# Attention and a two-layer network in one kernel: where the network's steps, the products with v and the weight sums stand

## The chip, the cores and the metric

The kernel runs on one core of one Trainium2 chip. The metric is the device time of one execution in microseconds (us), the median of several runs. The engines that matter here are PE (TensorE, the matrix products), DVE (VectorE), ACT (ScalarE), POOL (GpSimd) and SP (SyncE, which here only issues transfers, DMAs). Each has its own queue of instructions, runs it in the order in which it is written, and waits at semaphores for the others.

## The reference

Per batch (8) and head (8) an attention over 576 tokens of 64 values with a decay, then per token a normalised two-layer network of 512, 2048 and 512 values:

```python
scores = scale * np.matmul(q, k.transpose(0, 1, 3, 2))
decay = cum[:, :, :, None] - cum[:, :, None, :]      # cum: running sum of log f
scores = np.where(causal, -1000000000.0, scores + decay)
attn = np.exp(scores - np.max(scores, axis=-1, keepdims=True))
attn = attn / (np.sum(attn, axis=-1, keepdims=True) + 1e-09)
x = np.matmul(attn, v)                               # heads side by side: (8, 576, 512)
xn = (x - mu) / np.sqrt(var + 1e-06) * g_ln
return x + np.maximum(xn @ w_ch1, 0.0) @ w_ch2
```

## The kernel before

**Slots.** Attention is cut into 256 slots, four per head: slot u works on head u // 4 and on a block of 128 query rows, t = 1 to 4 (t = 1 takes a first block of 64 rows along, t = 0). In its slot a block gets its scores (`qk_mm`, PE, tiles s), its softmax (`softmax_a` on DVE, `softmax_e` on ACT, `normalise` on DVE and POOL, tile p) and, one slot later, a copy into another buffer by DMA (`move`, tile pq). `LAG_MOVED = 4` slots after the scores PE transposes the block (`transpose_unit`, tiles tr), ACT copies the result (`transposed_hi`, tile ph) and DVE the low part of it (`transposed_lo`, tile pl). The product with v (`av_unit`, tile o, from vv, ph and pl) covers two blocks at a time and stands one slot after the second one's transposes, t = 2 or t = 4. `finish` and `finish_add` write o to xs, and every second head's xs goes to DRAM (xa, xb). Heads 0 to 13 are handled with a shorter lag and in other orders.

**Steps.** The network works on chunks of 256 tokens, 18 of them. For the first `PLAIN_CHUNKS = 12` a chunk takes 16 steps, one per 128 hidden values: `mm1` (12 matmuls of 256 columns: four blocks of w1, each in high and low parts), `mm1_high` and `mm1_low` (ACT and DVE, tile hh), and `mm2` (6 matmuls of 512 columns), which stands in the next slot that is reached. A slot holds at most one step. From slot `EVEN_FROM = 70` on, `credit` spreads the steps that are left evenly over the slots that are left, so that some slots have none. `moe.limit` says which chunks' tokens are finished, and `Moe.fetch` loads and splits the next chunk (tiles xr, x) from 8 steps before it begins.

**Wide part.** The last six chunks are done after attention, as `WIDE = 3` times 512 tokens in `wide_part`, with 7 products for 8 in the first layer (`Wide.order`). They need sums and differences of blocks of w1; `weight_sums` makes these in 80 pieces (8 times 10; mostly POOL, some ACT), the last piece of each ten being `keep`: four stores to DRAM (sd) on SP. One piece stands in every slot from `SUMS_FROM = 120`. `wide_start` loads and prepares the first 512 tokens, in the last five slots, which have no scores any more.

**Order.** All queues are written by hand: a slot runs the letters of a string in `ORDERS`, from slot 56 on `WwAthQFlMSPNgreamLRDBZ`. A is the product with v, the transposes and the scores, dealt among each other by `dealt`; h and l are the copies of the transposes; M is `mm1`, N is `mm2` of the step before; S, e and B are the softmax; F and a finish o; P prepares a coming head (casts, subtractions and the loads kl, raw, vr, and xq, whose rows come from the cast); R is `moe.rest` (loads and splits of chunks); D is `move`; Z a piece of the sums. PSUM has six banks in rotation for tr, s, o, h and xp.

Of the kernel before, what the change touches and what calls it, by code (L numbers as in the profile page):

```python
# [31 lines left out]
LAG, LAG_MOVED = 2, 4  # L32
MOVED = 14
PLAIN_CHUNKS = 12
WIDE = (NCHUNK - PLAIN_CHUNKS) // 2
PAIRS = FT // 2
EVEN_FROM = 70
SUMS_FROM = 120
# [27 lines left out]
def attn_moe(ctx: ExitStack, tc: tile.TileContext, qk, v, f, g, w1, w2, out):  # L66
# [387 lines left out]
    def transpose_unit(h, t):  # L454
        n = f"{h.n}"
        pt = rows_of(h, t)
        work_, todo = [], []

        def tr(out_, in_):
            m = in_.shape[0]  # L460
            if in_.dtype == F32R:
                todo.append(lambda: nc.tensor.transpose(out_.bitcast(F32R), in_, identr[:m, :m]))  # L462
            else:
                todo.append(lambda: nc.tensor.transpose(out_, in_, ident[:m, :m]))

        if t <= 2:
            if t == 1:
                h.ph1 = work.tile([P, 704], F32 if h.full else F32R, tag="ph1", bufs=1, name=f"ph1_{n}")
                h.pl1 = None if h.full else late.tile([P, 384], F32R, tag="pl1", bufs=1, name=f"pl1_{n}")
            ph = h.ph1  # L470
            pl = ph if h.full else h.pl1
            tp = bank(f"tr{n}_{t}")
            if t == 1:
                tr(tp[0:64, 0:128], rows_of(h, 0)[:, 0:D])
                tr(tp[0:64, 64:192], pt[:, 0:64])
                tr(tp[:, 192:320], pt[:, 64:192])
                work_.append((tp[0:64, 0:192], ph[0:64, 0:192], ph[64:128, 0:192]))
                work_.append((tp[:, 192:320], ph[:, 320:448], pl[:, 0:128]))
            else:
                tr(tp[0:64, 0:128], pt[:, 0:64])  # L480
                tr(tp[:, 128:256], pt[:, 64:192])
                tr(tp[:, 256:384], pt[:, 192:320])
                work_.append((tp[0:64, 0:128], ph[0:64, 192:320], ph[64:128, 192:320]))
                work_.append((tp[:, 128:384], ph[:, 448:704], pl[:, 128:384]))
        else:
            if t == 3:
                h.ph2 = work.tile([P, 9 * P], F32 if h.full else F32R, tag="ph2", bufs=1, name=f"ph2_{n}")
                h.pl2 = None if h.full else late.tile([P, 7 * P], F32R, tag="pl2", bufs=1, name=f"pl2_{n}")
            c = 0 if t == 3 else P
            ph = h.ph2[:, : 8 * P].rearrange("p (k c) -> p k c", k=4)[:, :, c : c + P]  # L490
            pl = None if h.full else h.pl2[:, : 6 * P].rearrange("p (k c) -> p k c", k=3)[:, :, c : c + P]
# [4 lines left out]
            work_.append((tp[0:64, 0, :], ph[0:64, 0, :], ph[64:128, 0, :]))  # L496
            work_.append((tp[:, 1:4, :], ph[:, 1:4, :], pl))
            if t == 4:
                tp = bank(f"tr{n}_4b")[:, :P]
                tr(tp, pt[:, 64 + 3 * P : 64 + 4 * P])  # L500
                work_.append((tp, h.ph2[:, 8 * P :], None if h.full else h.pl2[:, 6 * P :]))
        h.parts = work_
        return todo

    def transposed_hi(h, t):
        for tp, hi, lo in h.parts:
            nc.scalar.copy(out=hi, in_=tp)  # L507
# [58 lines left out]
    def dealt(t, u1, a, b, q):  # L566

        if t == 4 and q:
            return a[:5] + a[8:] + b[:2] + q[:1] + a[5:6] + b[2:] + q[1:2] + a[6:7] + q[2:3] + a[7:8] + q[3:]
        if t == 4:  # L570
            return a[:5] + a[8:] + b[:2] + a[5:6] + b[2:] + a[6:8]
        if t == 2:
            return a[:3] + a[4:] + b + a[3:4] + q
        return (a + b if u1 else b[1:] + b[:1]) + q
# [386 lines left out]
    def wide_start(u):  # L961

        w, k = wides[0], u - (len(slots) - LAG_MOVED - 1)
# [138 lines left out]
    slots += [None] * (LAG_MOVED + 1)  # L1102
# [14 lines left out]
    for u, slot in enumerate(slots):  # L1117
# [7 lines left out]
        def turn(more):  # L1125

            for lag in (LAG, LAG_MOVED):
                b = before(lag + more)
                if b is not None and hd[b[0]].lag == lag:
                    return b  # L1130
            return None

        av, av_t = None, 0
        if turn(1) is not None and turn(1)[1] in (2, 4):
            av, av_t = hd[turn(1)[0]], turn(1)[1]
# [11 lines left out]
        def piece(c):  # L1147
            tu = turn(0)
# [36 lines left out]
            elif c == "R":  # L1185
                moe.limit = min(PLAIN_CHUNKS, max(0, u - (LAG if u < 4 * MOVED else LAG_MOVED) - 1) // (4 * H) * S // C)
# [24 lines left out]
            elif c == "Z":  # L1211
                if u >= SUMS_FROM and sum_todo:
                    sum_todo.pop(0)()
                if slot is None:
                    wide_start(u)

        def prep():
# [13 lines left out]
            first = turn(0)  # L1231
# [4 lines left out]
            second = turn(1)  # L1236
# [5 lines left out]
    moe.limit = PLAIN_CHUNKS  # L1242
    while moe.left() > 0:
# [7 lines left out]
        moe.rest()  # L1251
    for _ in range(W2_LOW):
# [41 lines left out]
```

## Time and profile before

| | |
|---|---|
| device time, median of 3 runs | 1218.45 us (1218.02 to 1218.68) |
| the profiled execution | 1218.54 us, of which 1216.8 us from its first to its last instruction (the span) |
| PE busy | 1176.7 us, 97% of the span |
| DVE, ACT, POOL busy | 812.9, 669.8, 521.5 us (67%, 55%, 43%) |
| DMA | 249.62 MB, 205 GB/s in the mean |
| mean granted TensorE clock | 0.988 of full speed |

A matmul's end is modelled, so busy shares of PE also cover time in which it is only filling; what a matmul occupies is read from the starts of two that follow each other. Waits are idle time of an engine before an instruction, with the instruction or DMA that ended it. Where time is read from a timeline, the first number is the start in us from the span's start and the second the duration shown.

### The profile page before, as it was taken

To read this page: it belongs to the slowest core of one execution; us is meant where nothing else is said; L and a number is where in the kernel's file an instruction comes from. 1 tells how busy PE (TensorE), PEld (TensorE's weight loads), DVE (VectorE), ACT (ScalarE), POOL (GpSimd) and SP (SyncE) were. 2 spreads that over 40 slices of the span, in tenths; PEclk is the share of its full clock that TensorE was granted. 3 is DMA by queue.
4 is the path that set the end of the run, shared out by engine and by line. 5 is a ranking of instruction groups with operands and counts; after the bars stand their busy time and mean duration, and the time that the engine had idled before them with its cause. 6 is when DMAs were issued, how large, how long until landed. Compare 5 with 4: busy or idle time off the path is not lost. (4 is left out here: it accounts for less than half of the span.)

```text
span 1216.8 us, 26138 instructions
## 1 busy us (share of the span) xinstructions
PE 1176.7 (97%) x7996; PEld 1040.8 (86%) x7996; DVE 812.9 (67%) x2935; ACT 669.8 (55%) x1981; POOL 521.5 (43%) x633
## 2 busy tenths in 40 slices
PE   7998999999999999999999999999999999999998
PEld 5666889989898998888888888889998899898997
DVE  5787646676868777686777768686776635536433
ACT  5887645565666666566566666666664322223221
POOL 3568543444444556655665664444442202002000
PEclk8998999999999999999999999999999999999999
DMA  6778654666666677767777677667765646545542
GB/s 202 226 241 265 204 160 142 198 219 206 219 219 222 216 232 232 217 210 245 234 244 250 214 239 251 197 200 247 214 201 152 227 142 190 191 149 182 173 139 95
DMA packets 181916, 249.62 MB, mean 205 GB/s; under 512 B 39952, under 2 KB 111632, under 8 KB 181776
## 3 DMA queue, kind: packets, MB, share of 16 engines
q1 hardware_dynamic: 181776, 247.95, 64.7%
q8 instruction: 64, 1.05, 0.4%
q14 instruction: 76, 0.62, 0.1%
HBM read 166.90 MB, written 31.75 MB: 163 GB/s over the span
## 5 line engine op out<-in xcount | busy, mean ns | idle before, releaser
L428 POOL TENSOR_SCALAR p<-p,st 64x64 f32<-64x64 f32 (+4 forms) x320 | 172.1, 542 | 403.4 <-DVE st L427 156.4
L421 ACT ACTIVATE p<-p,st 64x64 f32<-64x64 f32 (+4 forms) x320 | 178.6, 559 | 117.9 <-DVE st L410 93.5
L634 PE MATMUL h<-x,w1h 128*128 128x256 f32 x768 | 222.3, 289 | 3.3 <-DVE xs L602 1.8
L635 PE MATMUL h<-x,w1h 128*128 128x256 f32 x768 | 218.7, 285 | 0.6 <-DVE x L619 0.3
L636 PE MATMUL h<-x,w1l 128*128 128x256 f32 x768 | 217.7, 283 | 0.0
L634 PEld LDWEIGHTS h<-x,w1h 128*128 128x128 f32 x768 | 146.9, 191 | 8.0 <-DVE xs L602 2.9
L507 ACT CAST ph<-tr 64x128 fp32r<-64x128 f32 (+4 forms) x416 | 117.3, 331 | 64.9 <-PE tr L462 43.9
L656 PE MATMUL acc<-w2h,hh 128*128 128x512 f32 x384 | 152.0, 396 | 0.0
L657 PE MATMUL acc<-w2s,hh 128*128 128x512 f32 x384 | 151.5, 395 | 0.0
L658 PE MATMUL acc<-w2h,hh 128*128 128x512 f32 x384 | 150.9, 393 | 0.0
L635 PEld LDWEIGHTS h<-x,w1h 128*128 128x128 f32 x768 | 147.1, 192 | 2.3 <-DVE x L619 1.5
L636 PEld LDWEIGHTS h<-x,w1l 128*128 128x128 f32 x768 | 147.1, 192 | 0.0
L410 DVE CUSTOM_DVE_ANT_0 p<-s,mask 64x64 f32<-64x64 f32 (+4 forms) x320 | 130.3, 420 | 19.7 <-DMA pq<-p 8.1
L642 ACT ACTIVATE hh<-h 128x256 fp32r<-128x256 f32 x192 | 73.6, 383 | 112.1 <-PE h L636 110.9
L1061 POOL TENSOR_TENSOR c<-u,s 128x256 f32<-128x256 f32 x24 | 17.7, 737 | 223.4 <-DVE u L1060 223.4
L512 DVE TENSOR_TENSOR ph<-tr,ph 64x192 fp32r<-64x192 f32 x208 | 62.6, 301 | 74.8 <-ACT ph L507 70.7
L374 PE MATMUL s<-hi 128*64 128x64 f32 x336 | 103.5, 314 | 4.0 <-DVE st L410 1.7
L647 DVE SCALAR_TENSOR_TENSOR hh<-h,hh 128x256 fp32r<-128x256 f32 x192 | 80.5, 419 | 33.1 <-ACT hh L642 31.5
L374 PE MATMUL s<-kl,xq 66*64 66x64 f32 x336 | 96.4, 291 | 3.8 <-DMA xq<-hi 3.6
L512 DVE TENSOR_TENSOR pl<-tr,ph 128x128 fp32r<-128x128 f32 x208 | 95.3, 458 | 4.6
L462 PE MATMUL tr<-identr,pq 128*128 128x128 f32 (+1 forms) x700 | 93.4, 233 | 2.9 <-DMA pq<-p 2.9
L658 PEld LDWEIGHTS acc<-w2h,hh 128*128 128x128 f32 x384 | 72.4, 189 | 16.5
(146 smaller groups left out, 2951.2 us busy)
## 6 DMA issues: line engine op xcount, KB each, us to landing
w2s<-w2d SPq DMA_DIRECT2D x192, 256.0 KB
raw<-in_qk_dram SPq DMA_DIRECT2D x56, 576.0 KB
s<-sd SPq DMA_DIRECT2D x96, 256.0 KB
wr<-in_w_dram SPq DMA_DIRECT2D x32, 512.0 KB
pq<-p SPq DMA_DIRECT2D x50, 288.0 KB
wide<-w2d SPq DMA_DIRECT2D x48, 256.0 KB
pq<-p SPq DMA_DIRECT2D x50, 224.0 KB
vr<-in_v_dram SPq DMA_DIRECT2D x64, 160.0 KB
```

What stands on the lines that cost most here:

```text
L374: todo.append(lambda: nc.tensor.matmul(*a, **k))
L410: nc.vector.tensor_tensor_reduce(out=pt[:m, a:z], in0=sp, in1=mask[:m, off + a : off + z], scale=-SCALE, scalar=3.0e38 if i == 0 else st[: ...
L421: nc.scalar.activation(pt[:m, :w], pt[:m, :w], AF.Exp, bias=st[:m, i : i + 1], scale=-1.0, accum_out=st[:m, 2:3])
L428: nc.gpsimd.tensor_scalar(out=pt[:m, :w], in0=pt[:m, :w], scalar1=st[:m, 3:4], scalar2=1.0, op0=ALU.mult, op1=ALU.mult)
L507: nc.scalar.copy(out=hi, in_=tp)
L512: nc.vector.tensor_tensor(out=lo, in0=tp, in1=hi.bitcast(F32), op=ALU.subtract)
L634: mm(ph, w1h[:, k, fs], c.x[k][:, 0, :], start=(k == 0), stop=False)
L635: mm(ph, w1h[:, k, fs], c.x[k][:, 1, :], start=False, stop=False)
L636: mm(ph, w1l[:, k, fs], c.x[k][:, 0, :], start=False, stop=(k == KT - 1))
L656: mm(c.acc[i], h[:, 0, ts_], w2h[:, j, :], start=(j == 0), stop=False)
L657: mm(c.acc[i], h[:, 0, ts_], low, start=False, stop=False)
L658: mm(c.acc[i], h[:, 1, ts_], w2h[:, j, :], start=False, stop=(j == FT - 1))
```

## The change

Fourteen chunks instead of twelve are done in steps, and two times 512 tokens instead of three by seven products. A step stands in every slot whose chunk is ready (`EVEN_FROM = 1000` is never reached). The product with v stands three slots after the second transposes instead of one (`AV_MOVED = 3`); the cast of v (`prep_v`), its load and the limit of the chunks move two slots with it, the loop gets two more slots at its end, and ph and pl are allocated where they are written (`places`) and no longer where the transposes stand, since the product with the old ones now stands in that same slot. `dealt` mixes the matmuls of a slot in other ways. The sums of w1 begin in slot 92 and stand in every second slot. `wide_start` moves from the last slots to the steps that are left after the loop.

```diff
 W2_WAIT = 2
 ALL = 2 * NCHUNK * FT + W2_WAIT
 LAG, LAG_MOVED = 2, 4
+AV, AV_MOVED = 1, 3
 MOVED = 14
-PLAIN_CHUNKS = 12
+PLAIN_CHUNKS = 14
 WIDE = (NCHUNK - PLAIN_CHUNKS) // 2
 PAIRS = FT // 2
-EVEN_FROM = 70
-SUMS_FROM = 120
+EVEN_FROM = 1000
+SUMS_FROM = 92
...
+    def places(h, t):
+
+        n, tp = f"{h.n}", h.banks[0]
+        if t == 1:
+            h.ph1 = work.tile([P, 704], F32 if h.full else F32R, tag="ph1", bufs=1, name=f"ph1_{n}")
+            h.pl1 = None if h.full else late.tile([P, 384], F32R, tag="pl1", bufs=1, name=f"pl1_{n}")
+        if t == 3:
+            h.ph2 = work.tile([P, 9 * P], F32 if h.full else F32R, tag="ph2", bufs=1, name=f"ph2_{n}")
+            h.pl2 = None if h.full else late.tile([P, 7 * P], F32R, tag="pl2", bufs=1, name=f"pl2_{n}")
...
+        return out_
+
     def transposed_hi(h, t):
+        h.parts = places(h, t)
         for tp, hi, lo in h.parts:
...
     def dealt(t, u1, a, b, q):
 
-        if t == 4 and q:
-            return a[:5] + a[8:] + b[:2] + q[:1] + a[5:6] + b[2:] + q[1:2] + a[6:7] + q[2:3] + a[7:8] + q[3:]
         if t == 4:
-            return a[:5] + a[8:] + b[:2] + a[5:6] + b[2:] + a[6:8]
+            return a[:5] + a[8:] + b[:1] + a[5:6] + b[1:2] + a[6:7] + b[2:3] + a[7:8] + b[3:] + q
+        if t == 2 and q:
+            return a[:3] + a[4:] + b[:2] + q[:1] + a[3:4] + b[2:] + q[1:]
         if t == 2:
-            return a[:3] + a[4:] + b + a[3:4] + q
-        return (a + b if u1 else b[1:] + b[:1]) + q
+            return a[:3] + a[4:] + a[3:4] + b
+        return (b if u1 else b[1:] + b[:1]) + q
 
...
-    def wide_start(u):
-
-        w, k = wides[0], u - (len(slots) - LAG_MOVED - 1)
+    def wide_start(k):
+
+        w = wides[0]
         if k == 0:
...
-    slots += [None] * (LAG_MOVED + 1)
+    slots += [None] * (LAG_MOVED + AV_MOVED)
...
-        def turn(more):
-
-            for lag in (LAG, LAG_MOVED):
-                b = before(lag + more)
+        def turn(more, more_moved):
+
+            for lag, k in ((LAG, more), (LAG_MOVED, more_moved)):
+                b = before(lag + k)
                 if b is not None and hd[b[0]].lag == lag:
                     return b
             return None
 
         av, av_t = None, 0
-        if turn(1) is not None and turn(1)[1] in (2, 4):
-            av, av_t = hd[turn(1)[0]], turn(1)[1]
+        ready = turn(AV, AV_MOVED)
+        if ready is not None and ready[1] in (2, 4):
+            av, av_t = hd[ready[0]], ready[1]
...
-                moe.limit = min(PLAIN_CHUNKS, max(0, u - (LAG if u < 4 * MOVED else LAG_MOVED) - 1) // (4 * H) * S // C)
+                last = LAG + AV if u < 4 * MOVED else LAG_MOVED + AV_MOVED
+                moe.limit = min(PLAIN_CHUNKS, max(0, u - last) // (4 * H) * S // C)
                 moe.rest()
...
-                if u >= SUMS_FROM and sum_todo:
+                if u >= SUMS_FROM and u % 2 == 0 and sum_todo:
                     sum_todo.pop(0)()
-                if slot is None:
-                    wide_start(u)
 
...
-            first = turn(0)
+            first = turn(0, 2)
             if first is not None and first[1] == 1:
                 m = first[0]
                 if not hd[m].full:
                     prep_v(hd[m])
-            second = turn(1)
+            second = turn(1, 3)
             if second is not None and second[1] == 1 and second[0] + 1 < B * H:
                 load_v(hd[second[0] + 1])
 
...
-    moe.limit = PLAIN_CHUNKS
+    moe.limit, steps = PLAIN_CHUNKS, 0
     while moe.left() > 0:
         if moe.can(2 * FT):
             moe.first()
         moe.fetch_low(ALL)
         moe.second()
         moe.rest()
+        wide_start(steps)
+        steps += 1
+    for k in range(steps, 5):
+        wide_start(k)
```

The first place is on PE, head 45's first product with v (tiles o45_2, from ph1_45 and pl1_45). Before:

```order
L519 MATMUL o45_2_10608<-ph1_45_10469,vv45_10521 128x320
L519 MATMUL o45_2_10608<-ph1_45_10469,vv45_10521 128x256
L519 MATMUL o45_2_10608<-ph1_45_10469,vv45_10521 128x128
L519 MATMUL o45_2_10608<-pl1_45_10470,vv45_10521 64x128
L462 MATMUL tr45_3_10611<-identr_74,pq45_3_10462 64x128
L462 MATMUL tr45_3_10611<-identr_74,pq45_3_10462 128x128 x3
L519 MATMUL o45_2_10608<-pl1_45_10470,vv45_10521 64x256
L374 MATMUL s46_3_0_10612<-hi46_10268 128x448
```

and now:

```order
L534 MATMUL o45_2_11085<-ph1_45_10832,vv45_10994 128x320
L534 MATMUL o45_2_11085<-ph1_45_10832,vv45_10994 128x256
L534 MATMUL o45_2_11085<-ph1_45_10832,vv45_10994 128x128
L534 MATMUL o45_2_11085<-pl1_45_10833,vv45_10994 64x128
L463 MATMUL tr46_1_11086<-identr_74,pq46_0_10940 64x128
L463 MATMUL tr46_1_11086<-identr_74,pq46_1_10942 64x128
L375 MATMUL s47_0_0_11087<-hi47_10859 64x64
L534 MATMUL o45_2_11085<-pl1_45_10833,vv45_10994 64x256
L463 MATMUL tr46_1_11086<-identr_74,pq46_1_10942 128x128
L375 MATMUL s47_0_0_11087<-kl47_10860,xq9_1294 64x64
L375 MATMUL s47_1_0_11088<-hi47_10859 128x192
```

Before, it stood with the transposes of its own head's next block, one slot after those of the last block that it reads; now the next head's first block is transposed there, and three slots lie between.

The second place is on SP, around the load xq of head 33 (tile xq9_1294). Before:

```order
L443 DMA pq32_0_7122<-p0_0_214 128x64
L443 DMA pq32_1_7124<-p32_1_7039 128x192
L850 DMA sd0_127<-wh0_6937 128x2x256
L850 DMA sd0_127<-sl0_0_6993 128x2x256
L850 DMA sd0_127<-wh0_6937 128x2x256
L850 DMA sd0_127<-sl0_1_7075 128x2x256
L750 DMA w2s83_7133<-w2d3_138 128x512
L357 DMA xq9_1294<-hi33_7042 64x576
```

and now:

```order
L444 DMA pq32_0_7242<-p0_0_214 128x64
L444 DMA pq32_1_7244<-p32_1_7170 128x192
L765 DMA w2s88_7249<-w2d8_143 128x512
L358 DMA xq9_1294<-hi33_7173 64x576
L444 DMA pq32_2_7310<-p32_2_7227 128x320
L865 DMA sd1_128<-wh1_6954 128x2x256
L865 DMA sd1_128<-sl1_0_7071 128x2x256
L865 DMA sd1_128<-wh1_6954 128x2x256
L865 DMA sd1_128<-sl1_1_7199 128x2x256
L765 DMA w2s89_7319<-w2d9_144 128x512
L338 DMA vr32_7357<-in_v_dram 128x320
```

The four stores of sums (sd) stood ahead of this xq, with one load between; now a set of four stands behind an xq, as all eight sets do, and the sets are twice as far apart in slots.

The third place is on PE, where chunk 2 begins (its first hidden tile is h2_0), around the scores of head 18. Before:

```order
L374 MATMUL s18_0_0_3598<-hi18_3404 64x64
L519 MATMUL o16_4_3594<-pl2_16_3502,vv16_3410 64x256
L462 MATMUL tr17_1_3597<-identr_74,pq17_1_3493 128x128
L374 MATMUL s18_0_0_3598<-kl18_3405,xq8_1151 64x64
L519 MATMUL o16_4_3594<-pl2_16_3502,vv16_3410 64x256
L374 MATMUL s18_1_0_3599<-hi18_3404 128x192
L519 MATMUL o16_4_3594<-pl2_16_3502,vv16_3410 64x256
L374 MATMUL s18_1_0_3599<-kl18_3405,xq8_1151 128x192
L634 MATMUL h2_0_3623<-x2_0_3540,w1h_124 128x256
```

and now:

```order
L375 MATMUL s18_0_0_3568<-kl18_3391,xq8_1151 64x64
L375 MATMUL s18_1_0_3569<-hi18_3390 128x192
L375 MATMUL s18_1_0_3569<-kl18_3391,xq8_1151 128x192
L463 MATMUL tr17_2_3625<-identr_74,pq17_2_3522 128x128 x2
L463 MATMUL tr17_2_3625<-identr_74,pq17_2_3522 64x128
L375 MATMUL s18_2_0_3626<-hi18_3390 128x320
L375 MATMUL s18_2_0_3626<-kl18_3391,xq8_1151 128x320
L534 MATMUL o16_4_3655<-ph2_16_3493,vv16_3506 128x256 x4
L534 MATMUL o16_4_3655<-ph2_16_3493,vv16_3506 128x128
L534 MATMUL o16_4_3655<-pl2_16_3494,vv16_3506 64x128
```

The first step of the chunk stood right behind the scores s18_1 of slot 72; now it is the one of slot 74, and slots 71, 72 and 73 have neither `mm1` nor `mm2`. From there to slot 255 one more slot, 106, lacks an `mm1`; before, 28 slots did between slot 80 and slot 255.

## Rows read from the trace of the kernel before

**Rows 1.** the page, part 1: busy time and instructions by engine

```profile
PE 1176.7 (97%) x7996; PEld 1040.8 (86%) x7996; DVE 812.9 (67%) x2935; ACT 669.8 (55%) x1981; POOL 521.5 (43%) x633
```

**Rows 2.** PE's waits, 199 to 932 us: us in total, times, longest

```profile
PE o L519 <- DVE ph L512: 8.3, 8, 2.3
PE s L374 <- DMA xq<-hi: 3.6, 4, 1.4
PE tr L462 <- DMA pq<-p: 2.9, 4, 0.9
...
PE s L374 <- DVE st L410: 1.7, 4, 0.8
PE s L374 <- DVE pl L512: 1.3, 3, 0.5
```

**Rows 3.** PE's waits, 932 us to the end

```profile
PE o L519 <- DVE ph L512: 1.4, 2, 1.0
PE wide L996 <- ACT xp L900: 1.4, 1, 1.4
```

**Rows 4.** stretches: length, busy PE PEld DVE ACT POOL (instructions), clock, DMA

```profile
199.00:255.00 56.00, 56.00 (x403) 51.54 (x403) 37.33 (x151) 32.07 (x97) 23.87 (x30) 1.00 0.62 194
451.00:750.00 299.00, 285.09 (x2047) 258.35 (x2046) 221.52 (x848) 185.62 (x563) 183.65 (x219) 0.99 0.73 233
```

**Rows 5.** timeline of PE, one step: start, duration, instruction

```profile
926.61 0.29 PE L634 MATMUL h<-x,w1h 128*128 128x256 f32 x1
...
929.43 0.46 PE L679 MATMUL xp<-identr,xw 128*128 128x128 f32 x4
```

**Rows 6.** timeline of PE, starts of the second and third 512 tokens

```profile
1038.45 0.28 PE L996 MATMUL wide<-xp,w1h 128*128 128x256 f32 x1
...
1124.09 0.28 PE L996 MATMUL wide<-xp,w1h 128*128 128x256 f32 x1
```

**Rows 7.** timelines of PE, then of DVE, at a slot without a step

```profile
671.62 0.28 PE L636 MATMUL h<-x,w1l 128*128 128x256 f32 x1
673.41 0.80 PE L519 MATMUL o<-ph,vv 128*128 128x256 f32 x5 [1.50 <-DVE ph L512]
...
670.90 1.28 DVE L709 TENSOR_SCALAR rs<-rs 128x2 f32<-128x2 f32 x1
672.22 0.16 DVE L710 TENSOR_TENSOR rs<-rs 128x2 f32<-128x2 f32 x1
```

**Rows 8.** timeline of PE between the chunks 1 and 2

```profile
254.30 0.37 PE L462 MATMUL tr<-identr,pq 128*128 128x128 f32 x3
254.51 0.25 PE L462 MATMUL tr_4b<-identr,pq 128*128 128x128 f32 x1
...
257.68 0.80 PE L519 MATMUL o<-ph,vv 128*128 128x256 f32 x5 [2.25 <-DVE ph L512]
...
258.89 0.22 PE L462 MATMUL tr<-identr,pq 128*128 128x128 f32 x1
258.95 0.20 PE L374 MATMUL s<-kl,xq 66*64 66x64 f32 x1
...
262.45 0.42 PE L462 MATMUL tr<-identr,pq 128*128 128x128 f32 x3
```

**Rows 9.** the stretch behind that wait, columns as in Rows 4

```profile
259.20:262.60 3.40, 3.40 (x18) 3.24 (x17) 2.04 (x11) 2.78 (x8) 0.69 (x1) 0.50 0.81 237
```

**Rows 10.** timelines of SP, then of PE, around the load xq of head 48

```profile
696.35 0.54 SPq L850 DMA_DIRECT2D sd<-wh  x1
...
699.84 0.61 SPq L357 DMA_DIRECT2D xq<-hi  x1
...
703.79 0.24 PE L374 MATMUL s<-kl,xq 66*64 66x64 f32 x1 [0.64 <-DMA xq<-hi]
```

**Rows 11.** timeline of PE behind eight loads of chunk rows (xw)

```profile
516.52 0.60 PE L679 MATMUL xp<-identr,xw 128*128 128x128 f32 x2 [0.69 <-DMA xw<-xb]
...
518.56 0.61 PE L462 MATMUL tr<-identr,pq 128*128 128x128 f32 x3 [0.87 <-DMA pq<-p]
```

More of the change, by code (lines that the diff above doesn't have):

```diff
@@ L456, in transpose_unit @@
         pt = rows_of(h, t)
-        work_, todo = [], []
+        todo = []
         def tr(out_, in_):
@@ L466, in transpose_unit @@
         if t <= 2:
[L467 to L471, printed above, removed]
             tp = bank(f"tr{n}_{t}")
@@ L476, in transpose_unit @@
                 tr(tp[:, 192:320], pt[:, 64:192])
-                work_.append((tp[0:64, 0:192], ph[0:64, 0:192], ph[64:128, 0:192]))
-                work_.append((tp[:, 192:320], ph[:, 320:448], pl[:, 0:128]))
             else:
@@ L482, in transpose_unit @@
                 tr(tp[:, 256:384], pt[:, 192:320])
-                work_.append((tp[0:64, 0:128], ph[0:64, 192:320], ph[64:128, 192:320]))
-                work_.append((tp[:, 128:384], ph[:, 448:704], pl[:, 128:384]))
-        else:
[L486 to L491, printed above, removed]
+            h.banks = [tp]
+        else:
             tp = bank(f"tr{n}_{t}").rearrange("p (k c) -> p k c", k=4)
@@ L495, in transpose_unit @@
                 tr(tp[:, k, :], pt[:, 64 + P * (k - 1) : 64 + P * k])
-            work_.append((tp[0:64, 0, :], ph[0:64, 0, :], ph[64:128, 0, :]))
-            work_.append((tp[:, 1:4, :], ph[:, 1:4, :], pl))
+            h.banks = [tp]
             if t == 4:
@@ L500, in transpose_unit @@
                 tr(tp, pt[:, 64 + 3 * P : 64 + 4 * P])
-                work_.append((tp, h.ph2[:, 8 * P :], None if h.full else h.pl2[:, 6 * P :]))
-        h.parts = work_
-        return todo
+                h.banks.append(tp)
+        return todo
+    def places(h, t):
[6 more added lines that the diff above has]
+            h.pl2 = None if h.full else late.tile([P, 7 * P], F32R, tag="pl2", bufs=1, name=f"pl2_{n}")
+        if t <= 2:
+            ph = h.ph1
+            pl = ph if h.full else h.pl1
+            if t == 1:
+                return [
+                    (tp[0:64, 0:192], ph[0:64, 0:192], ph[64:128, 0:192]),
+                    (tp[:, 192:320], ph[:, 320:448], pl[:, 0:128]),
+                ]
+            return [
+                (tp[0:64, 0:128], ph[0:64, 192:320], ph[64:128, 192:320]),
+                (tp[:, 128:384], ph[:, 448:704], pl[:, 128:384]),
+            ]
+        c = 0 if t == 3 else P
+        ph = h.ph2[:, : 8 * P].rearrange("p (k c) -> p k c", k=4)[:, :, c : c + P]
+        pl = None if h.full else h.pl2[:, : 6 * P].rearrange("p (k c) -> p k c", k=3)[:, :, c : c + P]
+        out_ = [(tp[0:64, 0, :], ph[0:64, 0, :], ph[64:128, 0, :]), (tp[:, 1:4, :], ph[:, 1:4, :], pl)]
+        if t == 4:
+            out_.append((h.banks[1], h.ph2[:, 8 * P :], None if h.full else h.pl2[:, 6 * P :]))
+        return out_
     def transposed_hi(h, t):
+        h.parts = places(h, t)
         for tp, hi, lo in h.parts:
@@ L1147, in piece @@
         def piece(c):
-            tu = turn(0)
+            tu = turn(0, 0)
             if c in "AtQ" and tu is not None and hd[tu[0]].lag == LAG_MOVED:
```

## The prediction, before the changed kernel was run

> **What bounds the kernel now.** I began with the busy times, where PE alone is near the span [rows 1], and went on to PE's waits, in attention from slot 56 on and in the rest [rows 2, 3]: they come to some 21 us there, and the largest entry is the product with v waiting for DVE's copy ph. Then I asked in which slots PE waits. In slots 56 to 70 every slot holds a step, and there PE is busy for 56.00 of 56.00 us while DVE has 37.33 and SP's transfers 0.62 of the DMA engines [rows 4]: a slot with a step covers every other engine. In 451 to 750 us, where about one slot in six has no step, PE lacks 13.9 us of 299, though no other engine is busier than 221.52 [rows 4]. So PE is the bound, its time is the sum of its matmuls and the holes, and nearly all holes are beside slots without a step. Such a hole: PE ends its step at 671.62 + 0.12, and the product with v begins at 673.41, shown as 1.50 idle behind DVE's copy [rows 7]; the copy had only one slot, and that one was short. The hole is really 1.67, since a matmul's shown end is late: every wait below costs 0.17 more than its row.
>
> **The change part by part.** The sum is made against the profiled execution, 1218.54 us; the median of the runs, 1218.45, is the same within 0.1.
>
> *Two plain chunks for one wide part: +5.7.* A step takes 929.43 - 926.61 = 2.82 us [rows 5], 32 of them 90.2, with 16 transposes of chunk rows at 0.07 [rows 8] 91.3. The wide part does the same tokens in 1124.09 - 1038.45 = 85.64 [rows 6], rows included. Both are PE without holes, so the 5.7 lie on the path.
>
> *Products with v three slots behind: -8.9.* The waits for ph are eight with 8.3 and two with 1.4 [rows 2, 3]; the one of 2.25 [rows 8] goes to the gap below, which leaves nine with 7.45 and 9 x 0.17 = 1.5 hidden. With two more slots, 7 us, the copies are done. What is late next: the copy of the new transposes into the same tiles has to wait for the product, but PE does that product in the same slot ahead of or among those transposes, and the copies need the transposes anyway, so this wait adds nothing. ACT, DVE, POOL and SP get no new instruction; the cast and subtraction of v move from slots t = 1 to t = 3. Bounds: -9 and -6.
>
> *A step in every slot: -3.5 for banks, -2 for other waits.* Scores that wait for a PSUM bank which DVE still reads cost 1.7 (four) and 1.3 (three) [rows 2], with the hidden part 4.2. The stretch with all steps has none, and of the 28 step-free slots behind slot 80 one is left. Of the waits for pq, 2.9 in four [rows 2], and of some like them at chunk starts, about half stand behind a step-free slot, where PE gained on SP by the 2.8 us that it had not to do; I take 2, bounds -4 and +3 (two chunks more bring two more starts).
>
> *The gap between chunks 1 and 2: +2.* The chunk's tokens are known finished two slots later, so slots 71 to 73 have no step where 71 alone had none. PE now goes from 254.30 to 262.45 there [rows 8], 8.15 us for about 3.9 of matmuls (a slot's attention is 56.00 / 15 - 2.82 = 0.9 in the mean [rows 4, 5], a t = 1 more; two of them and a `mm1`, half a step): 4.2 lost. In the new order four slots' attention, 3.7, stand ahead of the first step, which waits for: the product of head 15 and its store, the load of the first two blocks, their split, the load of the other two and their split. That chain ran before as well, beside two slots with steps which now are later. DVE has 37.33 / 15 = 2.5 us in a slot with a step [rows 4], without one some 2: four slots 8, against 3.7 of PE, so 4 to 5 us lost. Behind the wait of 2.25 the granted clock was 0.50, which is 1.2 GHz, for 3.40 us [rows 9], so that up to half of these, 1.7, comes on top, as it did before in the 4.2. In all 5 to 7, with a transfer more on the chain 9: +2, bounds 0 and +5.
>
> The Trainium skill speaks against this part: "TensorE: Matmul & The Clock Gate", section "HAM oscillation — how this bites in real kernels", says that an array left waiting goes back to half clock and starts the next burst cold each time. By that the longer gap costs a cold start; the trace agrees, rows 9 being one behind a wait. The sum is the same by both, as rows 9 are in it, and by the rule alone its upper bound would stand.
>
> *Sums from slot 92 in every second slot: -3.* They are off PE's path but for SP: the waits for xq are four with 3.6 [rows 2], 4.3 with the hidden part, and three of the four stand behind a set of four sd stores, as here: stores from 696.35, xq issued at 699.84, PE waiting at 703.79 [rows 10]. Now each set stands behind an xq and ahead of a pq that is needed three slots later. What hides the sums themselves is POOL's free time: 183.65 of 299 us with a piece in each slot [rows 4], less now. Bounds -4.3 and 0.
>
> *Other mixing in a slot: -3.* A transpose behind another takes (254.51 - 254.30) / 3 = 70 ns, one among products 60 [rows 8]; three more of a head's fifteen now stand among products, the score matmuls no longer do. Per head 0.03 to 0.1 us by these, 50 heads: bounds -5 and 0, and I take -3.
>
> *The end of attention: 0.* Two slots without scores more, all with steps; preparing the wide part moves into pure steps of 2.82 us. The first product needing prepared data waits 1.4 now [rows 3]; the loads and differences have some four steps, 11 us. Bounds -1.4 and +2.
>
> Sum: 5.7 - 8.9 - 3.5 - 2 + 2 - 3 - 3 = -12.7, or 1206 us.
>
> **The rivals.** *Transfers fall behind (slower).* From slot 107 on a chunk is 16 slots and begins at t = 4, so its rows (xw, 4 or 8 loads) always come in a t = 4 and a t = 2 slot, right behind the store of xs, on which SP waits, and ahead of xq. Where this happened once, eight loads wide, PE waited 0.69 and then 0.87 [rows 11]; with the hidden parts 1.9, and with 1.7 for a half clock as in rows 9 3.6. All ten chunks from there at 3.6 cost 36 and give 1242; four are the point from which it decides, 1206 + 14 = 1220. Against it: there PE had gained on SP in a step-free slot shortly before, and the same clusters in 199 to 255 us cost nothing [rows 4].
>
> *The holes move to DVE (a smaller gain).* DVE has 0.74 of 451 to 750 us [rows 4] and gets a step's work in every slot. If half the gain from v, banks and other waits comes back as waits for its low parts, 7 us: 1213. For it: short DVE instructions grow where POOL works, one of 128x2 to 1.28 against 0.16 [rows 7], and the sums last for twice as many slots. Against it: 37.33 of 56.00 us in rows 4 without a hole, and the pieces are as many as before. Were one such 1.1 us to reach PE in every head from 20 on, 44 x 1.1 = 48 would make it 1254; that end of it stands with the slower cases.
>
> Beside it the Trainium skill, "SBUF — State Buffer", section "Who interferes with whom", has this as a lock: a DVE instruction with two SBUF inputs or in a two-port mode stands still for the whole of the POOL instruction that came first. The 1.28 of rows 7 agrees.
>
> *More is gained.* If all terms lie at their lower bounds the sum is about -23: 1196.
>
> *It does not do what it says:* hardly open, since the order shows the steps in all slots but those named.
>
> **How the numbers follow.** The forecast, 1199 to 1212, has 0.62; the smaller gain, 1210 to 1216, 0.2; transfers or DVE on PE's path, 1216 to 1254, 0.1; more gain, 0.08. The range 1197 to 1215 leaves out about 2 in 10: most of the slower case and parts of the two others. What a measurement of this kernel can tell from no change is about 0.2%, 2.4 us, so 1216.0 divides: faster 0.84 (forecast, more gain, most of the smaller gain), same 0.07, slower 0.09.
>
> **What would show it.** In the changed profile: PE's waits for ph and pl near zero; PE busy as in the first of rows 4 from about slot 75 to 255; one long hole near 255 us with a half clock behind it; hardly a wait for xq; the steps in a wide part as long as in rows 6, and two of them. Wrong it would be by waits of PE for xq, xw or pq at each chunk, by waits for DVE in slots with a step, or by a long wait where the wide part begins.

## The result, and the profile after

The changed kernel took 1200.38 us (median of 4 runs, 1199.95 to 1200.71), the kernel before 1218.57 beside it; the ratio is 0.9844, with a 95% interval from 0.9829 to 0.986. A second measurement of both, on another chip, gave 0.9826 (0.9799 to 0.9853). That is 18 to 21 us less, where the sum gave 12.7: inside the range and inside the forecast of 1199 to 1212, near its lower end. One per cent is 12.2 us in what follows; ratios are always to the kernel before, measured on the same chip.

The profiled execution has a span of 1198.1 us. Its busy times stand in the page as in [rows 1]:

```profile
span 1198.1 us, 26041 instructions
...
PE 1174.0 (98%) x8044; PEld 1046.2 (87%) x8044; DVE 799.3 (67%) x2918; ACT 666.5 (56%) x1966; POOL 512.2 (43%) x621
```

PE has hardly less to do (1176.7 before): two plain chunks for a wide part cost it something, and what it loses are holes. Its waits from 199 to 932 us, as in [rows 2] (us in total, times, longest):

```profile
PE s L375 <- DVE pl L527: 1.4, 2, 1.1
PE o L534 <- DVE st L411: 1.2, 1, 1.2
PE h L649 <- DVE xs L617: 1.0, 4, 0.3
PE tr L463 <- DMA pq<-p: 1.0, 2, 0.6
PE o L534 <- POOL vv L366: 0.9, 1, 0.9
...
PE tr L463 <- PE o L534: 0.3, 1, 0.3
```

The wait for ph, 8.3 us before, is gone, that for xq too. From 932 us on the only one over 0.3 is the wide part's start, 1.7 where [rows 3] have 1.4. The stretches of [rows 4], and the gap between chunks 1 and 2 (columns as there):

```profile
199.00:255.00 56.00, 56.00 (x403) 51.52 (x402) 36.67 (x153) 31.63 (x96) 23.01 (x29) 1.00 0.61 193
451.00:750.00 299.00, 298.59 (x2180) 275.99 (x2179) 218.63 (x834) 182.03 (x550) 150.87 (x183) 1.00 0.71 224
255.00:270.00 15.00, 10.37 (x56) 8.20 (x54) 11.19 (x42) 9.30 (x29) 6.13 (x8) 0.77 0.66 216
260.30:267.10 6.80, 5.07 (x23) 4.56 (x22) 4.36 (x20) 5.16 (x17) 2.85 (x4) 0.50 0.81 262
```

The second row is the result: where PE lacked 13.9 of 299 us it now lacks 0.4, with about one slot in six filled that was empty before, and DVE, ACT and POOL are no busier than before. The third and fourth are what the change costs: in the gap PE stands for 4.6 of 15 us and has half clock (1.2 GHz) for 6.8. This varies: a second profiled execution of the same kernel has half clock for 13.7 us there (257.20 to 270.90). What it stands for is no longer one wait, as in [rows 8], but a row of them, in PE's timeline:

```profile
256.21 0.58 PE L534 MATMUL o<-ph,vv 128*128 128x320 f32 x3 [0.88 <-POOL vv L366]
...
258.25 0.21 PE L375 MATMUL s<-hi 128*64 128x64 f32 x1 [1.05 <-DVE pl L527]
...
259.55 0.40 PE L463 MATMUL tr<-identr,pq 128*128 128x128 f32 x3 [0.56 <-DMA pq<-p]
...
261.54 1.30 PE L534 MATMUL o<-ph,vv 128*128 128x256 f32 x5 [1.23 <-DVE st L411]
...
263.37 0.29 PE L463 MATMUL tr<-identr,pq 128*64 128x128 f32 x1 [0.42 <-DMA pq<-p]
```

Four slots of attention stand without a step in between, and four different things are late, one after the other: vv, pl, pq, st.

### The profile page after: what moved, and what is told of

Read it like the earlier page. It is cut to its first block, busy times and chain, and to the rows that moved or that the text cites. A ratio compares the mean times of both kernels' runs of the same rounds, so it can differ in the third digit from the quotient of the medians.

```text
span 1198.1 us, 26041 instructions
## 1 busy us (share of the span) xinstructions
PE 1174.0 (98%) x8044; PEld 1046.2 (87%) x8044; DVE 799.3 (67%) x2918; ACT 666.5 (56%) x1966; POOL 512.2 (43%) x621
## 3 DMA queue, kind: packets, MB, share of 16 engines
q8 instruction: 64, 1.05, 0.4%
## 4 chain that ended last, share of the span: by engine, by line
PE 72%; DVE 3%; DMA 2%; issue 1%; SPq 1%; ACT 0%; POOL 0%; DVEq 0%; ACTq 0%; POOLq 0%
PE h L649 7%; PE h L650 7%; PE h L651 7%; PE acc L671 7%; PE acc L672 7%; PE acc L673 7%; PE s L375 6%; PE o L534 6%; PE tr L463 3%; PE wide L1011 2%; PE wide L1013 2%; PE wide L1012 2%; PE wacc L1026 1%; PE wide L1027 1%; PE wide L1026 1%; PE wacc L1027 1%
## 5 line engine op out<-in xcount | busy, mean ns | idle before, releaser
L649 PE MATMUL h<-x,w1h 128*128 128x256 f32 x896 | 257.1, 287 | 2.1 <-DVE xs L617 1.0
L650 PE MATMUL h<-x,w1h 128*128 128x256 f32 x896 | 254.0, 283 | 0.9 <-DVE x L634 0.9
L651 PE MATMUL h<-x,w1l 128*128 128x256 f32 x896 | 253.2, 283 | 0.0
L671 PE MATMUL acc<-w2h,hh 128*128 128x512 f32 x448 | 176.3, 394 | 0.0
L672 PE MATMUL acc<-w2s,hh 128*128 128x512 f32 x448 | 176.1, 393 | 0.0
L649 PEld LDWEIGHTS h<-x,w1h 128*128 128x128 f32 x896 | 170.7, 191 | 5.9 <-DVE xs L617 2.0
L657 ACT ACTIVATE hh<-h 128x256 fp32r<-128x256 f32 x224 | 86.0, 384 | 161.0 <-PE h L651 159.1
L673 PE MATMUL acc<-w2h,hh 128*128 128x512 f32 x448 | 175.5, 392 | 0.0
L650 PEld LDWEIGHTS h<-x,w1h 128*128 128x128 f32 x896 | 170.8, 191 | 2.8 <-DVE x L634 1.7
L651 PEld LDWEIGHTS h<-x,w1l 128*128 128x128 f32 x896 | 170.6, 190 | 0.0
L662 DVE SCALAR_TENSOR_TENSOR hh<-h,hh 128x256 fp32r<-128x256 f32 x224 | 94.2, 420 | 48.8 <-ACT hh L657 45.4
L463 PE MATMUL tr<-identr,pq 128*128 128x128 f32 (+1 forms) x700 | 107.6, 227 | 1.4 <-DMA pq<-p 1.0
L463 PEld LDWEIGHTS tr<-identr,pq 128*128 128x128 f32 (+1 forms) x700 | 82.0, 130 | 14.8 <-DVE st L411 0.7
```

The source lines that it names most:

```text
L649: mm(ph, w1h[:, k, fs], c.x[k][:, 0, :], start=(k == 0), stop=False)
L650: mm(ph, w1h[:, k, fs], c.x[k][:, 1, :], start=False, stop=False)
L651: mm(ph, w1l[:, k, fs], c.x[k][:, 0, :], start=False, stop=(k == KT - 1))
L671: mm(c.acc[i], h[:, 0, ts_], w2h[:, j, :], start=(j == 0), stop=False)
L672: mm(c.acc[i], h[:, 0, ts_], low, start=False, stop=False)
L673: mm(c.acc[i], h[:, 1, ts_], w2h[:, j, :], start=False, stop=(j == FT - 1))
```

## The experiments

The question was which part of the change brought the gain. The prediction gave half of it to the longer way from transposes to products with v (the lag), and 5.5 us to the steps in every slot. The rival, called cover below: a slot without a step is short of everything at once, and a wait there that is taken away only uncovers the next. Where an expectation speaks of the record, the prediction above is meant.

**The lag undone.** The changed kernel with

```diff
-AV, AV_MOVED = 1, 3
+AV, AV_MOVED = 1, 1
-            first = turn(0, 2)
+            first = turn(0, 0)
-            second = turn(1, 3)
+            second = turn(1, 1)
```

> The changed kernel with the products with v one slot behind their transposes again (AV_MOVED 1), all else as changed; it undoes the lag alone. The theory of the record: the lag itself took away the waits for the copies ph, so they come back, up to 8.9 us, less the 2 that the gap between chunks 1 and 2 was priced at: about 1205 to 1207. The rival, cover: the copies were late only beside slots without a step, and there are almost none of those now, so one slot of lag is enough, no wait for ph comes back behind slot 75, and the gap between chunks 1 and 2 is shorter by two slots' limit: 1195 to 1199. By the rival, PE's waits from 199 us on have at most 1 us in products with v; by the record they have 6 or more.

Measured: 0.9844 (0.9819 to 0.9869), the same as the changed kernel. The waits for ph:

```profile
PE o L534 <- DVE ph L527: 3.0, 2, 2.6
```

They are two, at the two places where this kernel has slots without a whole step (in front of chunk 2, and at slots 104 and 105, which share one). Where steps stand, one slot of lag is enough. The gap got shorter, as the rival said; its stretch, columns as in [rows 4]:

```profile
255.00:270.00 15.00, 11.68 (x87) 10.30 (x86) 11.76 (x44) 9.28 (x30) 6.76 (x9) 1.00 0.73 236
```

From the last scores of slot 70 to those of slot 80 this kernel takes 38.3 us with eight steps in them, the changed kernel 37.0 with six: 4.3 us better at 2.82 a step. What it gains there it loses behind: a head's four slots take 15.57 us instead of 15.49, PE waits 1.5 us for a pq at 828.29, and there are 3.4 us of half clock behind slot 105.

**The change without its steps.** Twelve plain chunks and the even spread again; lag, sums and mixing as changed:

```diff
-PLAIN_CHUNKS = 14
+PLAIN_CHUNKS = 12
-EVEN_FROM = 1000
+EVEN_FROM = 70
```

(with the wide part's start in the last slots, as in the kernel before)

> The changed kernel with twelve plain chunks and the even spread of steps from slot 70 on, as before the change; the lag of three slots, the sums in every second slot and the mixing stay. It is the change without its steps. The record: lag -8.9, sums -3, mixing -3 and none of the +5.7, -5.5: about 1204, waits for ph gone, those for banks (some 4 us) left. The rival, cover: the slots without a step lose what they lost for several reasons at once, so with the copies out of the way the next late thing (scores behind a bank, low parts, first blocks behind pq or x) takes the place of part of it: 1208 to 1214. Both have about 15 to 20 us of holes less or more to show in the stretch 451 to 750 us, where before PE lacked 13.9 us: by the record about 5, by the rival 8 to 12.

Measured: 1.0079 (1.0055 to 1.0103), slower than the kernel before, and worse than either theory. Its waits, 199 to 932 us:

```profile
PE tr L463 <- DMA pq<-p: 7.5, 8, 2.0
PE s L375 <- DVE pl L527: 4.6, 8, 1.0
PE h L649 <- DVE xs L617: 2.2, 9, 0.3
...
PE s L375 <- DMA xq<-hi: 1.5, 1, 1.5
PE h L649 <- DVE pl L527: 1.4, 2, 0.9
```

No wait for ph is left, and the total is no smaller than in [rows 2]: pq and pl have taken its place. One such place, in SP's timeline (start, duration, instruction),

```profile
517.56 0.38 SPq L682 DMA_DIRECT2D xw<-xa  x1
...
522.06 0.43 SPq L682 DMA_DIRECT2D xr<-xa  x1
522.59 0.47 SPq L444 DMA_DIRECT2D pq<-p  x1
...
523.79 1.11 SPq L444 DMA_DIRECT2D pq<-p  x2
```

in PE's,

```profile
523.05 0.28 PE L651 MATMUL h<-x,w1l 128*128 128x256 f32 x1
525.18 0.43 PE L463 MATMUL tr<-identr,pq 128*128 128x128 f32 x3 [1.85 <-DMA pq<-p]
```

and the stretch behind it, columns as in [rows 4]:

```profile
527.00:530.00 3.00, 3.00 (x14) 2.90 (x14) 2.29 (x9) 0.70 (x3) 1.67 (x3) 0.50 0.57 200
```

Ten loads of chunk rows hold SP for 4.9 us (517.56 to 522.49), the pq behind them go out late, PE waits 1.85 us and then works at half clock. This is the prediction's slower rival, transfers that fall behind, but it comes beside slots without a whole step (141 has no `mm1`, 142 no `mm2`) and not in the changed kernel.

**The same with the lag undone too.** So only the slower sums and the new mixing are left of the change:

```diff
-AV, AV_MOVED = 1, 3
+AV, AV_MOVED = 1, 1
```

(and `turn` as in the lag undone)

> The changed kernel with twelve plain chunks, the steps spread evenly from slot 70 as before, and the products with v one slot behind again: the kernel before with the sums in every second slot from 92 and the new mixing only. It differs by the lag alone from the one that has lag and even spread, which was at a ratio of 1.008. The record: without the lag the waits for ph are back, 8.9 more than that one: ratio 1.015. The rival: with empty slots the lag itself does harm (the wait for ph is only replaced by waits for pq, low parts and first blocks, and the gap gets longer), so that this one is faster than that one by 5 to 10 us: ratio 1.000 to 1.004.

Measured: 0.9983 (0.9964 to 1.0001), the same as the kernel before: without the steps, the slower sums and the new mixing together gain nothing that can be told from noise. It has more waits for ph than any other kernel here,

```profile
PE o L534 <- DVE ph L527: 10.3, 12, 2.6
```

and still is 0.96%, 11.7 us, faster than the one with the lag, which has none; the rival gave 5 to 10. This pair is the lag alone beside empty slots: it takes 10.3 us of waits for ph away and loses 11.7 us. The largest part I can name is the clock: between 200 and 1000 us, in windows of 2 us, PE has half clock for 23.8 us in the kernel with the lag and for 3.4 in the one without, up to 10 us of loss. All runs of the two point the same way: their mean granted clock is 0.981 to 0.986 with the lag, 0.987 to 0.994 without.

**The steps alone.** The kernel before with

```diff
-PLAIN_CHUNKS = 12
+PLAIN_CHUNKS = 14
-EVEN_FROM = 70
+EVEN_FROM = 1000
```

and with the wide part's start in the last steps, as in the change.

> The kernel before with the steps alone: fourteen plain chunks, a step in every slot from the first on, the wide part's start moved into the last steps as in the change. One slot of lag for the products with v, sums of w1 in every slot from 120, and the old mixing stay. The record: +5.7 for the swap, -3.5 and -2 for banks and other waits, the waits for ph staying or going in part: 1211 to 1219. The rival, cover: nearly all holes go with the empty slots, those behind ph too, and what is left is what the old rate of the sums costs: 1203 to 1208; waits for ph then are at most 3 us, all at the two places where the order still has empty slots (71 and 72, 105).

Measured: 0.9789 (0.977 to 0.9808), faster than the whole change and than both theories had it. Its waits in attention:

```profile
PE o L519 <- DVE ph L512: 2.7, 2, 2.2
PE s L374 <- DMA xq<-hi: 2.0, 1, 2.0
PE h L635 <- DVE st L426: 0.8, 1, 0.8
```

Of 9.7 us for ph 2.7 are left, in the gap and behind slot 105; xs, xw, pl and the banks are gone with the steps alone. So cover holds: the steps bring all of the gain, and the other three parts together take 0.4 to 0.55% of it away.

**Empty slots in a row.** Twelve plain chunks, used up as they come, so that slots 236 to 255 have no step:

```diff
-PLAIN_CHUNKS = 14
+PLAIN_CHUNKS = 12
```

(with the wide part's start in the last slots, as in the kernel before)

> The changed kernel with twelve plain chunks, which are used up as early as they come: a step in every slot to 235, and then twenty slots in a row without one, where the kernel before has them one in six. The wide parts are three, as before, so 5.7 less of step time. If a slot without a step costs the same wherever it stands (some 21 us for 28 of them before, 0.76 each), 1200 - 5.7 + 15: 1208 to 1212. The rival: an empty slot beside full ones costs less, since the engines behind PE catch up in between; in a row PE has some 1 us of work a slot and DVE some 2, so each costs 1.1 or more, and half clock comes on top: 1216 to 1235.

Measured: 1.0176 (1.0155 to 1.0197), the slowest of all and slower than even the rival had it; 5.6 us of that are a wait for loads of sums at the wide part's start. The twenty slots:

```profile
906.00:963.00 57.00, 38.04 (x193) 31.82 (x192) 39.64 (x164) 34.75 (x110) 32.83 (x43) 0.61 0.52 164
```

That is 3.0 us for a slot (57.5 us for 19 of them), with no engine busy for more than 40 of 57 us, and PE at a mean clock of 0.61. PE's waits there name pq (7.4 us), vv (5.2) and st (5.1): I take it that, alone, a slot is bound by the chain from scores to transposed probabilities, which no run tests. A full slot takes 15.49 / 4 = 3.87 us. A step of 2.8 us therefore costs no more than 0.9 us there: a slot left empty saves little of it.

**The old rate of the sums,** in the changed kernel:

```diff
-SUMS_FROM = 92
+SUMS_FROM = 120
-                if u >= SUMS_FROM and u % 2 == 0 and sum_todo:
+                if u >= SUMS_FROM and sum_todo:
```

> The changed kernel with the sums of w1 as they were, from slot 120 in every slot; all else as changed. The record gave the slower sums -3 us, since three of four waits for xq stood behind a set of stores of sums: about 1203 with waits for xq back, some 3 us of them behind slot 120. The rival: those waits came from PE's gain on SP in slots without a step, which are gone, so the sets of stores are hidden whatever their rate: 1199 to 1201, with no wait for xq.

Measured: 0.9893 (0.9871 to 0.9915), 0.5 to 0.7% slower than the changed kernel: more than the 3 us of the record. But little of the waiting is for xq as the record had it (1.4 us); 4.5 us are for pq, the longest at a chunk's start. POOL's timeline there,

```profile
533.09 1.44 POOL L351 TENSOR_TENSOR kl<-raw,hi 64x576 fp32r<-64x576 f32 x1
534.50 0.54 POOL L429 TENSOR_SCALAR p<-p,st 128x320 f32<-128x320 f32 x1
534.99 1.30 POOL L831 TENSOR_TENSOR wa<-w1h,w1l 128x512 f32<-128x512 f32 x1
```

SP's queue in its waits from 526 to 542 us,

```profile
SPq L444 <- POOL wa L831: 1.3, 1, 1.3
```

SP's timeline,

```profile
528.55 0.47 SPq L444 DMA_DIRECT2D pq<-p  x1
529.07 0.59 SPq L865 DMA_DIRECT2D sd<-wh  x1
...
530.85 0.51 SPq L865 DMA_DIRECT2D sd<-sl  x1
...
535.01 2.97 SPq L444 DMA_DIRECT2D pq<-p  x2
```

and PE's:

```profile
540.58 0.45 PE L463 MATMUL tr<-identr,pq 128*128 128x128 f32 x3 [2.81 <-DMA pq<-p]
...
580.62 0.24 PE L375 MATMUL s<-kl,xq 66*64 66x64 f32 x1 [1.36 <-DMA xq<-hi]
```

Two things hold the pq up. A set of four stores of sums (sd) takes 2.3 us of SP's queue between the first pq and the next, and SP waits 1.3 us with a pq behind POOL's sums (wa), which stand among its instructions for kl, p and hi. The fourth pq is issued 11.2 us behind the last scores of slot 140, in the changed kernel, where no set stands there, 6.5. The wait for xq, too, stands behind a set of stores, in SP's timeline

```profile
575.89 0.45 SPq L865 DMA_DIRECT2D sd<-sl  x1
...
577.19 0.64 SPq L358 DMA_DIRECT2D xq<-hi  x1
```

as in [rows 10]. The two waits with the hidden 0.17 of each, 4.5 us, and the half of 3.4 us at half clock behind the first come to 6 us, about what this kernel loses.

**The transposes in one row,** in the changed kernel:

```diff
-            return a[:5] + a[8:] + b[:1] + a[5:6] + b[1:2] + a[6:7] + b[2:3] + a[7:8] + b[3:] + q
+            return a[:5] + a[8:] + b + a[5:8] + q
...
-            return a[:3] + a[4:] + b[:2] + q[:1] + a[3:4] + b[2:] + q[1:]
+            return a[:3] + a[4:] + b + a[3:4] + q
```

> The changed kernel with the transposes of a head in one row behind the large products with v instead of one by one among the small ones; the score products follow as they do in the changed kernel. The record gave the mixing -3 us (bounds -5 and 0): 1203, up to 1205. The rival: a small product behind a short transpose takes about as much longer as the transpose takes less, so that mixing gains nothing or loses: 1196 to 1200; its four slots' PE time without holes in a head would be under the changed kernel's 15.53 us (3.90, 3.35, 4.44, 3.84).

Measured: 0.9841 (0.982 to 0.9863), the same, and the four slots of a head are no shorter than in the changed kernel. Interleaving one by one gains nothing against a row; this does not tell yet how the old mixing stands to the new, which the last experiment does.

**The gap filled.** The changed kernel with three slots held back earlier:

```diff
+HOLD = (48, 56, 64)
-        want = moe.can(wp.ready()) and u >= FIRST_MOE
+        want = moe.can(wp.ready()) and u >= FIRST_MOE and u not in HOLD
```

> The changed kernel with no step in the slots 48, 56 and 64, so that the 32 steps of the first two chunks last three slots longer and only one slot in front of chunk 2 (instead of four rows without a step, 71 to 74 by the order) is empty; nothing else moves. The gap between chunks 1 and 2 costs some 9.4 us in the changed kernel, half clock for 6.8 us in it included. If a slot without a step costs what it lacks of cover for itself, some 0.7 each, the cost only spreads out and the gap keeps about 3: 1194 to 1197, ratio to before 0.979 to 0.982, no half clock at 260 us. The rival, that the gap's chain (product of head 15, store, load, split, load, split) sets it and not the number of empty slots: the chain still takes its time, 1198 to 1202.

Measured: 0.9752 (0.9731 to 0.9773), 0.7 to 0.9% better than the changed kernel, more than expected. The gap, 6 us earlier now, as a stretch of 15 us again:

```profile
249.00:264.00 15.00, 14.40 (x105) 12.74 (x104) 13.34 (x54) 10.24 (x32) 6.31 (x8) 1.00 0.85 258
```

PE lacks 0.6 us where it lacked 4.6, at full clock. The last score product of slot 80 starts at 279.9 us, in the changed kernel at 289.6, with the same 38 steps done in both: the gap is worth 9.7 us (8.9 against the second execution of the changed kernel), and the three empty slots, each by itself and earlier, cost nothing that can be seen.

**The changed kernel again,** beside the two that follow:

> The changed kernel once more, beside the two that follow on the same chip. By its first interval its ratio to before is 0.983 to 0.986, behind the steps alone, which measured 0.979; if that order was a difference of chips, this one comes out at 0.979 too.

Measured: 0.9826 (0.9799 to 0.9853), so the order of the changed kernel and the steps alone (0.9789) stands, though the intervals touch.

**Steps, held slots, and the two rates of the sums.** The kernel with the steps alone, and

```diff
+HOLD = (50, 60)
-        want = moe.can(wp.ready()) and u >= FIRST_MOE
+        want = moe.can(wp.ready()) and u >= FIRST_MOE and u not in HOLD
```

once so, and once with the slower sums too.

> The same with the sums as in the kernel before, from slot 120 in every slot; against the steps alone only the two held slots are new. The gap between chunks 1 and 2 cost 4.9 us there with 3.4 us of half clock in it, and 2.3 in the changed kernel with three slots held: 2 to 3 us less than the steps alone, ratio 0.976 to 0.978. If the sums' rate is worth 3 us as the record says, 0.2% slower than the one above; if it matters only beside the lag of three, where it measured 6 us, as fast.

> The steps alone (lag of one slot, old mixing), with no step in the slots 50 and 60, so that one slot in front of chunk 2 is empty instead of two, and the sums of w1 from slot 92 in every second slot. If the lag is worth nothing once the steps cover, this is as fast as the changed kernel with held steps: ratio 0.973 to 0.977, some 1189. The record's lag term would make it slower than that by up to 9 us, 0.982. By the record the slower sums make it 3 us faster than the next one.

Measured: 0.9742 (0.9719 to 0.9765) with the old rate, 0.9744 (0.9716 to 0.9772) with the slower one. With a lag of one the rate of the sums is worth nothing: it only changes which wait is left. With the old rate it is

```profile
PE s L375 <- DMA xq<-hi: 1.5, 1, 1.5
```

(1.4 to 2.0 us in each of the four kernels here that have the old rate and fourteen chunks in steps, 6 to 8 us behind the first store of a set), and with the slower one

```profile
PE tr L463 <- DMA pq<-p: 2.3, 2, 1.8
```

of which the 1.8 follow a set and six loads of chunk rows. Both are as fast as the changed kernel with held slots: lag, sums and mixing can all be left as they were. These three are the fastest kernels of the study, some 1190 us, 9 us under the changed kernel.

**The mixing alone.** The kernel with steps, two held slots and the old sums, with the changed kernel's order of transposes, products and scores in a slot.

> The steps alone with two held slots (lag of one slot, old rate of the sums), and in it the changed kernel's way to mix a head's transposes, products with v and scores; the order within a slot is all that is new. The record gave the mixing -3 us: ratio 0.972. The rival: the four slots of a head took 15.57 us without holes in the two kernels with lag one and the new mixing, and 15.42 and 15.43 in the two with the old; 0.14 for each of 46 heads is 6 us the other way: ratio 0.979, and the fastest slots of a head come to 15.57 again.

Measured: 0.9782 (0.9758 to 0.9805), 0.4% or 4.9 us slower than without it, as the rival said; the two intervals together make that good to some 4 us. The four slots of a head, the fastest of each, come to 15.58 us in PE's timeline, where the kernels with the old order have 15.42 and 15.43; the changed kernel, with the lag of three, has 15.49.

## Why the prediction was right, and where it was not

The forecast held because its largest terms had the wrong owner and the right sign. That their sum came so near is in part luck: the steps were worth some 25 us more than forecast, and lag, sums and mixing some 18 less. By the experiments, in us:

| term | forecast | measured | by |
|---|---|---|---|
| two plain chunks for a wide part | +5.7 | +5.7 | kept; not measured by itself |
| a step in every slot | -5.5 | about -31 | steps alone, -25.7 with the swap in it |
| products with v three slots behind, with the gap | -6.9 | 0 with steps, +11.7 without | lag undone, in either setting |
| of it the gap between chunks 1 and 2 | +2 | +4 to +6 | stretches of the traces, slots 70 to 80 |
| slower sums | -3 | 0, or -6 beside the lag | sums at two rates |
| other mixing | -3 | +5 with lag one, +3 beside the lag | mixing alone; slots of a head |
| end of attention | 0 | 0 | start of the wide part |

The longer gap comes from the lag (the limit of the chunks moves with it) and goes with it when the lag is undone, so the 0 holds it and it is not added again. Summed by the experiments (steps, mixing and sums with a lag of one, then the lag itself): 5.7 - 31 + 5 + 0 + 0 = -20, where 18 to 21 were gained. Each row is good to some 3 us.

- *What bounds the kernel:* right, and it was the better guide than the sum. The sentence that a slot with a step covers every other engine was read from [rows 4], and the changed kernel's 298.59 of 299 us is that sentence.
- *Two plain chunks for one wide part:* as costed, as far as the trace shows: a step takes 2.81 us behind attention (1012.94 to 1015.75), and from the wide part's start at 1018.56 to the end are 179.5 us, 2.0 of them waits, against 178.4 from the corresponding start in [rows 6].
- *Products with v:* the step that failed. It took the nine waits for ph as the price of the lag and asked what is late next only for the copies themselves. The whole attention of an empty slot is late next: with the lag and without the steps, pq takes 7.5 us and pl 6.0. That a wait names ph means only that ph came last. With a step in every slot nothing of the nine waits is left to take away, and the term is worth nothing.
- *A step in every slot:* mis-sized by the same error, the other way round. It was given what waits were left over when ph and xq had been handed out. The row that has the right size stood in [rows 4]: 13.9 us in 299 missing. From slot 80 to 255 (290.55 to 931.89 us) PE lacked 20.3 us before, two stretches of 3.4 us at half clock cost up to 3.4 (only a third one, [rows 9], was in the sum), and the hidden 0.17 of some thirty holes makes 5: 29 in all. The steps alone still lack 3.8 us there and have one such stretch, so some 24 of the 31 have a name and the rest has none.
- *The gap:* the mechanism and the place were right, the size at its upper bound of +5. The half clock was put at up to 1.7 us, as in [rows 9]; it lasted 6.8 instead of 3.4, and 13.7 in the second execution. A slot's attention was read a little short, 0.9 us; a full slot less its step is 3.87 - 2.82 = 1.05. The Trainium skill, "TensorE: Matmul & The Clock Gate", section "HAM oscillation — how this bites in real kernels", has an array that waits go back to half clock and start its next burst cold. By that rule alone the upper bound would have stood. The trace agrees with the rule here, and not everywhere: with the lag undone PE waits 2.55 us at the same place and keeps full clock (the row 255.00:270.00 of that kernel).
- *Sums:* the mechanism was right in part, the size held in neither setting. Stores of sums do hold up what stands behind them on SP, with steps in all slots too: every kernel here with fourteen chunks in steps and the old rate keeps one wait for xq behind a set. But the steps alone took 3.6 us of such waits to 2.0, and with a lag of one the slower rate has a wait for pq in their place, so it gains nothing. Beside the lag of three it gains 6 us, through SP's stores and POOL's sums ahead of a pq. Why the later load and cast of v make that so was not tried.
- *Mixing:* wrong in sign. Only the transposes were priced, 70 and 60 ns, not the products and scores between which they were put. By slots, the mixing alone has 0.05 us more up to the scores of t = 1 and 0.08 more up to those of t = 4; which products they go to is open.
- *The rivals:* the terms' lower bounds add up to -22, not -23; the 1196 stands. Transfers did not fall behind in the changed kernel, where no wait for xw or xq is left, but they do where steps are missing (the wait at 525.18 above) and, with the old rate of the sums, with all steps too (540.58 above). The holes did not move to DVE, though more of its short instructions grew: 21 of 130 such instructions took over 0.3 us, 12 of 117 before. In the changed kernel, from 300 to 932 us (count, then ns min/median/max):

```profile
L722 DVE TENSOR_TENSOR rs<-rs x30: 140/161/1312, 321.4 to 897.6; 128x2 f32<-128x2 f32 x30
L723 DVE TENSOR_TENSOR rs<-rs,sv x30: 160/161/1348, 321.6 to 897.8; 128x2 f32<-128x2 f32 x30
```

Up to 1.35 us for 0.16, which is no longer than the longest before (1.35); the mean of the first is 351 ns where the same instruction before had 253. The Trainium skill, "SBUF — State Buffer", section "Who interferes with whom", calls it a lock between DVE and POOL. The trace agrees: each of the 21 ends within 0.05 us of the end of an instruction of POOL. It costs next to nothing here: from 451 to 750 us PE lacks 0.4 us in all.

## What to carry to other kernels

When an engine that should be the bound has holes, look first at where they stand, not at what each wait names: if they all stand in places of one kind, the thing to change is the place. A wait's last releaser is one of several that are nearly as late, so its total is a price only if nothing else in the slot is late behind it; compare a stretch with the holes and one without them for the real one. And empty slots apart are cheaper than empty slots in a row: three together cost some 9 us here, and the same three apart, early in attention, nothing that could be seen. Apart is not always free: the 28 single ones of the kernel before cost PE 20.3 us, 0.7 each, half clock not counted.

## What was not expected of the hardware

Half clock can follow a wait of a microsecond or two in the middle of work. Behind the wait of 1.85 us PE had it from 527 to 530 us (the row above), so that the wait cost nearly twice its row. In the kernel with the lag and without the steps, 10.2 of the 23.8 us of half clock stand in the gap, and the rest behind four waits of 1.2 to 2.0 us. But it does not follow each: a wait of 2.55 us in the lag undone, and one of 2.15 (at 784.44 us) in the change without its steps and lag, were followed by none. Three of the four kernels with held slots have none at all from 200 to 1000 us. With attention alone on it PE has a mean clock of 0.61 over 57 us, though it is busy for two thirds of the time.
